# Loading the second batch's q and k ahead of a quarter of w_out, and transposing them in earlier slots

## The chip, the cores and the metric

The kernel runs on one core of a Trainium2 chip. The metric is the time of the whole kernel on the device in microseconds (us), as the median of several runs. The engines are named as the profile names them: PE is the TensorE matmul and PEld its weight load, DVE is VectorE, ACT is ScalarE, POOL is GpSimd and SP is SyncE. The last two mostly issue DMAs here.

## What is computed

Attention with a sliding window over 8 batches, 8 heads, 576 positions and a head size of 64, followed by a two-layer network with a piecewise activation on the 8 x 576 = 4608 tokens:

```python
scores = np.matmul(q, k.transpose(0, 1, 3, 2)) / np.sqrt(D)
mask = np.abs(pos[:, None] - pos[None, :]) <= 32
attn = softmax(np.where(mask, scores, -1e9))
x = np.matmul(attn, v).transpose(0, 2, 1, 3).reshape(B * S, H * D)   # 4608 x 512
h = x @ w_in                                                         # 512 x 2048
g = np.where(h >= 1, h, np.where(h <= -1, 0.0, (h + 1) ** 2 / 4))
out = g @ w_out                                                      # 2048 x 512
```

Inputs and output are float32; the matmuls take bfloat16, into which the loads cast.

## The kernel before, in words

All instructions are emitted by one Python program in a fixed order (`tc.manual_schedule()`), and each engine works through its own in that order. The order of the work is written by hand in the loop at L495, whose steps are called slots here. In slot `a` below 72, PE projects one tile of 256 tokens onto 256 of the 2048 columns of w_in (`project`, L486: 8 matmuls into a PSUM tile `hp`), ACT and DVE apply the activation and leave the result in `gT` (L532 to L540), and then PE does what else is planned for this slot: attention steps (`run(a)`), parts of the output product, and `run(a + 0.5)`. There are 8 slots to a token tile: slots 0 to 7 are tile 0, slots 8 to 15 tile 1, and slot 16 begins tile 2, the first whose `xT` holds tokens of the second batch.

Attention steps are put into slots by `at(a, ...)`. For one batch they are: `tposes` transposes q and k on PE, from the tiles `qn` and `kn` as loaded into PSUM tiles `tp`, which are then copied into `qT` and `kT`; `scores` (L213) adds the mask's bias by matmuls with `ident` (slots before 14), multiplies k and q and takes the exp on ACT into `pt`; `sums` (L267) multiplies the weights with v and with ones, takes the reciprocal by ln and exp on ACT, and leaves a multiply on DVE to be done at the next `flush`, which writes `xT`. PSUM tiles for these steps come from two pools, `ps_s` and `ps_n`, of one two-bank buffer each; `hp` has two buffers, so slot a needs the buffer of slot a-2. From the third batch on, q and k are transposed by DMAs on SP's queue (`xpose`), and only batches 0 and 1 use PE for it.

The activation has two forms. As a rule ACT does a relu into `rr`, DVE a maximum of `hp` and `rr`, and DVE a last operation; `hp` is free after the maximum. In slots of `two_on_act` (L382) ACT does relu and square, and DVE's single last operation (L537) reads `hp`, which is free only after that.

The first two token tiles use w_out in two halves of 256 columns, since w_out arrives late. The list `pairs` (L381) names the slot and the piece: piece x is half x//8 of the columns, tile x%8//4, and quarter x%4 of the 2048 rows (`pair`, L456: 8 matmuls). Pieces 0 to 3 are the left half of tile 0, piece 3 the last that needs w_out's rows k = 12 to 15 in blocks of 128. When four pieces are done ACT copies the sum to `osb` (L469) and SP stores it.

All loads but the first q are issued by POOL in the order of the `put` lists (L150 to L159). They use 8 semaphores in turn, so that a load waits at its issue until the load eight places earlier has landed.

`tposes(b, (t, half), (t, half))` (L325) makes four groups of transposes in two PSUM tiles. Each tile has two parts, of 5 and of 4 transposes per head pair (copies of 640 and of 512 columns). Before, ACT copies the first part of each tile and DVE the second.

Of the kernel before, what the change touches and what calls it, by code (L numbers as in the profile page):

```python
# [14 lines left out]
def kernel(  # L15
# [40 lines left out]
    ps_s = ctx.enter_context(tc.tile_pool(name="ps_s", bufs=1, space=bass.MemoryType.PSUM))  # L56
    ps_n = ctx.enter_context(tc.tile_pool(name="ps_n", bufs=1, space=bass.MemoryType.PSUM))
# [17 lines left out]
    V, P, A = nc.vector, nc.gpsimd, nc.scalar  # L75
# [68 lines left out]
    def put(todo):  # L144
        for fn, *x in todo:
            fn(*x)
# [2 lines left out]
    w = [(load_w_in, c0, c1, h) for c0, c1 in zip(cuts, cuts[1:]) for h in range(2)]  # L149
    put(w[:4] + [(load_half, 1, t, h) for t in range(2) for h in range(2)] + w[4:12])  # L150
    put([(load_w_out, 0, 0, 4)] + w[12:])
    put([(load_w_out, 0, k, k + 4) for k in range(4, 16, 4)] + [(load_rows, 1, t) for t in range(2)])
    put([(load_v, 1, n) for n in range(4)])
    P.tensor_copy(band[HD[1], 0:128], band[HD[1], 64:192])
    for m, n, x in ((mask4, 8, 128), (mask8, 4, TAIL)):
# [8 lines left out]
    def qkT(b, t):  # L164
        if t == 0:
            return qTs[b % 3][:, PAD:]
        if b not in kT:
            kT[b] = ktp.tile([128, NY * S], BF, name="kT")
        return kT[b]

    def tpose(b, n, t, copy, ps):


        half, part = divmod(n, 2)
        j0, j1 = ((0, 5), (5, 9))[part]
        if b:
            src = qn[b] if t == 0 else kn[b]
            src = [src[:, half + 2 * h] for h in range(2)]
            dst = qkT(b, t).rearrange("d (y e p j) -> d y e p j", y=2, e=2, j=9)[:, half, :, :, j0:j1]
            like = "d j (e p) -> d e p j"  # L180
        else:
            src = (qn, kn)[t][b, half]
            src = src if src.shape[1] == 9 else [src[:, h] for h in range(2)]
            dst = qkT(b, t).rearrange("d (y l p j) -> d l y p j", l=2, p=32, j=9)[:, half, :, :, j0:j1]
            like = "d j (p y) -> d y p j"
        for j in range(j0, j1):
            if isinstance(src, list):
                for h in range(2):
                    nc.tensor.transpose(ps[HD[h], j - j0], src[h][:, D * j:D * j + D], ident)  # L189
            else:  # L190
                nc.tensor.transpose(ps[:, j - j0], src[:, j], ident)
        return lambda: copy(dst, ps[:, :j1 - j0].rearrange(like, p=64 if b else 32))
# [132 lines left out]
    def tposes(b, *sets):  # L325

        todo = []
        for (t, half), pool in zip(sets, (ps_s, ps_n)):
            tp = pool.tile([128, 2, 8, 128], BF, name="tp", tag="bb")
            todo += [tpose(b, 2 * half + part, t, (A.copy, V.tensor_copy)[part], tp[:, part]) for part in range(2)]  # L330
        for copy in todo:
            copy()

# [44 lines left out]

    NB = NT // TB
    NF = DFF // 256  # L380
    pairs = [(6, 0), (7, 1), (8, 2), (9, 3), (11, 4), (12, 5), (15, 6), (15, 8), (16, 7), (17, 9)]  # L381
    two_on_act = (1, 7, 8, 9, 10, 11, 12)  # L382
    ev = {}

    def at(a, *todo):


        ev.setdefault(a, []).extend(x for x in todo if x)

    def steps(b, cut):  # L390

        for k, (lo, hi) in enumerate(((0, cut), (cut, MAIN))):
            for y1 in range(2):
                yield (sums, b, y1, lo, hi), (scores, b, (y1, y1 + 1), (0, 2), (2 * k, 2 * k + 2))
        yield (sums, b, 0, MAIN, S), (scores8, b)

    at(1, (tposes, 0, (0, 1), (1, 1)))
    at(2, (scores, 0, (0, 1), (0, 2), (2, 4)), (scores8, 0, ps_o))
    at(3, (scores, 0, (1, 2), (0, 2), (2, 4), ps_n), (sums, 0, 0, TB, MAIN, ps_s))
    at(4, (sums, 0, 1, TB, MAIN))  # L400
    at(5, (sums, 0, 0, MAIN, S, ps_s))
    seq = [x for b in range(1, B) for x in steps(b, 224)]
    at(13, seq[0][1])
    at(13.5, (*seq[1][1], ps_n))
    at(14, (*seq[0][0], ps_s), seq[1][0])
    at(16, seq[2][1])
    for n, a in enumerate((18, 20, 26.5, 28)):
# [5 lines left out]
    for n, a in enumerate(sl):  # L413
        at(a, seq[6 + n][0], seq[7 + n][1] if n < len(sl) - 1 else None)
    for t in range(2):
        at(11 + t, (tposes, 1, (t, 0), (t, 1)))
    loads, xps = {}, {16: [(2, 0)], 18: [(2, 1)]}
    for b in range(LONG + 1, B):
        a = sl[5 * (b - 1) - 7] - 17
# [53 lines left out]
    def run(pos):  # L473
        todo = []
        for fn, *x in ev.get(pos, []):
            if fn is sums:
                todo.append(sums(*x))
            elif fn is tposes:
                tposes(*x)
            else:  # L480
                pool = (x.pop(),) if x[-1] in (ps_s, ps_n, ps_o) else ()
                fn(*x, eng, *pool)
        for end in todo:
            end()
# [10 lines left out]
    for a in range(NF * NB + 2 * NF):  # L495
# [11 lines left out]
        if a < NF * NB:  # L507
            if wide:
                n, f = divmod(a - WIDE[0], 2 * NF)
                t = WIDE[0] // NF + 2 * n  # L510
# [6 lines left out]
            else:  # L517
                t, f = divmod(a, NF)
# [6 lines left out]
                elif not hps:  # L525
                    pool, tag = (ps_o, "op") if a == 6 else (ps_h, "hp")
# [60 lines left out]
```

The softmax here doesn't subtract the row's maximum and nothing guards it: scores larger than these inputs give would overflow.

## Time and profile before

| | us |
|---|---|
| median of 6 runs | 308.28 (307.87 to 308.71) |
| the profiled execution, its own time | 308.26 |
| its span, first to last instruction | 306.5 |
| PE busy | 298.1 (97%) |
| DVE busy | 240.4 (78%) |
| ACT busy | 191.5 (62%) |
| POOL busy | 77.0 (25%) |

The granted clock of TensorE is 0.999 of full speed over the span. The stretch of the change lies between 20 us (where POOL issues the loads concerned) and 47 us (slot 16). DMA queues are at 9 tenths or more in nearly every slice up to about 180 us and idle for most of the rest.

A timeline row gives start, length, engine, line, operation, output<-inputs, shape, the number of instructions merged into the row, and in brackets how long the engine stood idle before it and what released it. Lengths of neighbouring matmul rows overlap, since matmuls are pipelined; the distance from start to start is what a block costs. A row of the chain of waits gives start, length, and the instruction or wait on the path that set the end.

### The profile page before, as it was taken

How to read it: one execution, taken by the hardware profiler on the slowest of the kernel's cores; microseconds unless marked ns; L12 is line 12 of the kernel's file. 1: busy time of each engine (PE TensorE's matmuls, PEld its weight loads, DVE VectorE, ACT ScalarE, POOL GpSimd, SP SyncE). 2: the span in 40 equal slices, each digit the busy share in tenths (PEclk: the TensorE clock that was granted, in tenths of full speed). 3: DMA queues.
4: the chain of work that ended last, by engine and by line, in shares of the span. 5: the costliest groups of instructions: out<-in, count | busy, mean ns of one | idle time of the engine just before them, and what ended most of it. 6: DMA issues, size and time to landing. Idle time of an engine off the chain costs nothing.

```text
span 306.5 us, 7974 instructions
## 1 busy us (share of the span) xinstructions
PE 298.1 (97%) x3388; PEld 181.0 (59%) x3388; DVE 240.4 (78%) x376; ACT 191.5 (62%) x320; POOL 77.0 (25%) x92
## 2 busy tenths in 40 slices
PE   8889999999999999999999999999999999999995
PEld 3467778877666676666654544444445444446644
DVE  4278568888888989998999998888888888788700
ACT  3687886738856756776766766665667654444311
POOL 8797651037009009004600900000000000000000
PEclk9999999999999999999999999999999999999999
DMA  9999999999999999998999992550101000000121
GB/s 152 184 197 199 182 200 151 174 157 159 142 186 105 183 171 121 164 148 109 154 119 174 135 159 45 111 114 34 36 34 37 36 34 35 36 34 34 59 80 68
DMA packets 137171, 35.67 MB, mean 116 GB/s; under 512 B 122160, under 2 KB 132912, under 8 KB 137136
## 3 DMA queue, kind: packets, MB, share of 16 engines
q0 software_dynamic: 102976, 18.06, 83.5%
q1 hardware_dynamic: 34016, 16.81, 26.0%
q8 instruction: 26, 0.43, 0.6%
q10 hardware_dynamic: 144, 0.29, 0.4%
q14 instruction: 9, 0.07, 0.1%
HBM read 36.70 MB, written 9.44 MB: 151 GB/s over the span
## 4 chain that ended last, share of the span: by engine, by line
PE 90%; DMA 4%; POOL 3%; ACT 1%; issue 1%; DVE 0%; POOLq 0%; ACTq 0%
PE op L449 36%; PE hp L489 21%; PE hp L514 18%; PE bb L295 6%; PE op L464 4%; DMA w_in<-in_moe_w_in_dram 4%; PE bb L229 2%; POOL w_in L111 1%; PE op L440 1%; POOL vn L107 1%; PE tp L189 1%; ACT pt L237 1%; POOL kh L86 0%; DVE gT L537 0%; ACT mx L536 0%
## 5 line engine op out<-in xcount | busy, mean ns | idle before, releaser
L533 ACT ACTIVATE rr<-hp 128x512 f32<-128x512 f32 x144 | 85.6, 595 | 86.2 <-PE hp L489 41.8
L449 PE MATMUL op<-w_out,gT 128*128 128x512 bf16 x496 | 126.9, 380 | 0.0
L539 DVE TENSOR_TENSOR mx<-hp,rr 128x512 f32<-128x512 f32 x137 | 94.4, 689 | 25.7 <-ACT rr L533 23.9
L540 DVE SCALAR_TENSOR_TENSOR gT<-rr,mx 128x512 bf16<-128x512 f32 x137 | 94.8, 692 | 4.7
L489 PE MATMUL hp<-xT,w_in 128*128 128x256 bf16 x640 | 83.1, 273 | 2.6 <-DMA w_in<-in_moe_w_in_dram 1.2
L489 PEld LDWEIGHTS <-w_in 128*128 128x128 bf16 x640 | 61.9, 98 | 23.0 <-issue 3.3
L449 PEld LDWEIGHTS <-gT 128*128 128x128 bf16 x496 | 46.1, 98 | 45.2
L514 PE MATMUL hp<-xT,w_in 128*128 128x512 bf16 x256 | 65.7, 379 | 0.0
L514 PEld LDWEIGHTS <-w_in 128*128 128x128 bf16 x256 | 25.1, 98 | 30.2
L99 POOL DMA_DIRECT2D qn<-in_q_dram x12 | 14.6, 1221 | 89.9 <-DMA kT<-kn 87.9
L237 ACT ACTIVATE pt<-bb 128x1024 bf16<-128x1024 f32 (+1 forms) x33 | 32.7, 1002 | 4.5 <-PE bb L229 3.1
L107 POOL DMA_DIRECT2D vn<-in_v_dram x32 | 27.5, 888 | 4.6 <-DMA w_out<-in_moe_w_out_dram 3.6
L307 DVE TENSOR_TENSOR xT<-bb,rc 128x512 bf16<-128x512 f32 (+1 forms) x32 | 21.0, 657 | 9.7 <-ACT rc L302 8.8
L453 ACT COPY osb<-op 128x512 f32<-128x512 f32 x31 | 18.0, 581 | 11.4 <-PE op L449 11.1
L302 ACT ACTIVATE rc<-lr 128x512 f32<-128x512 f32 (+2 forms) x40 | 23.5, 587 | 1.3
L301 ACT ACTIVATE lr<-bb 128x512 f32<-128x512 f32 (+2 forms) x40 | 22.0, 551 | 0.4 <-PE bb L295 0.4
L203 DVE TENSOR_TENSOR pt<-pt,mask 128x1024 bf16<-128x1024 bf16 (+1 forms) x33 | 20.3, 614 | 0.5 <-ACT pt L237 0.5
L295 PE MATMUL bb<-pt,ones 64*64 64x256 bf16 (+3 forms) x352 | 19.5, 255 | 0.1
L295 PE MATMUL bb<-pt,vn 64*64 64x128 bf16 (+3 forms) x712 | 18.4, 204 | 0.2 <-DMA vn<-in_v_dram 0.2
L295 PEld LDWEIGHTS <-ones 64*64 64x64 bf16 x352 | 10.3, 105 | 11.6 <-issue 11.6
L295 PEld LDWEIGHTS <-vn 64*64 64x64 bf16 x712 | 16.7, 107 | 0.4 <-DMA vn<-in_v_dram 0.4
L464 PE MATMUL op<-w_out,gT 128*128 128x256 bf16 x128 | 16.5, 273 | 0.0
(61 smaller groups left out, 140.2 us busy)
## 6 DMA issues: line engine op xcount, KB each, us to landing
out_dram<-osb SPq DMA_DIRECT2D x35, 256.0 KB, 2.3
vn<-in_v_dram POOLq DMA_DIRECT2D x32, 144.0 KB, 10.0
qn<-in_q_dram POOLq DMA_DIRECT2D x12, 288.0 KB, 6.3
kn<-in_k_dram POOLq DMA_DIRECT2D x12, 288.0 KB, 9.0
w_in<-in_moe_w_in_dram POOLq DMA_DIRECT2D x12, 128.0 KB, 5.5
w_out<-in_moe_w_out_dram POOLq DMA_DIRECT2D x4, 256.0 KB, 8.1
w_out<-in_moe_w_out_dram POOLq DMA_DIRECT2D x2, 512.0 KB, 13.2
kh<-in_k_dram POOLq DMA_DIRECT2D x4, 144.0 KB, 5.2
```

The source lines that it names most:

```text
L107: nc.gpsimd.dma_start(out=vn[b][64 * a:64 * a + 64, :, h], in_=v[b, y:y + 2].rearrange("y s d -> (y s) d") .rearrange("(c r) d -> r c d", ...
L237: A.activation(p, ps[:, :, :w * n].rearrange(like, y=m), AF.Exp, scale=D ** -0.5)
L295: nc.tensor.matmul(bb[HD[h], a, o + c0:o + c1], ones[HD[a]] if c is None else vn[b][HD[a], c, h], p(a, h), start=n == 0, stop=True, skip_g ...
L301: A.activation(lr[:, :, :D0], bb[:, :, D0:2 * D0], AF.Ln)
L302: A.activation(rc[:, :, :D0], lr[:, :, :D0], AF.Exp, scale=-1.0)
L449: nc.tensor.matmul(op[tt], gT[:, j, home(tt // 2), 128 * (tt % 2):128 * (tt % 2) + 128], w_out[:, j], start=j == 0, stop=j == 15)
L464: nc.tensor.matmul(o[:, tt], gT[:, j, p, 128 * tt:128 * tt + 128], w_out[:, j, 256 * half:256 * half + 256], start=not done, stop=len(done ...
L489: nc.tensor.matmul(hp[:, j], w_in[:, kk, 256 * f + 128 * j:256 * f + 128 * j + 128], xT[:, kk, r0:r0 + TB], start=first and n == 0, stop=l ...
L514: nc.tensor.matmul(hp.rearrange("p n t -> p (n t)"), w_in[:, kk, 128 * f:128 * f + 128], xT[:, kk, r0:r0 + 2 * TB], start=n == 0, stop=n == 3)
L533: A.activation(rr, hp, AF.Relu, scale=0.5, bias=0.5)
L539: V.tensor_max(mx, hp, rr)
L540: V.scalar_tensor_tensor(g, rr, 1.0, mx, op0=ALU.min, op1=ALU.mult)
```

## The change

It does five things:

1. POOL issues the second batch's q and k (`load_rows`) ahead of w_out's last quarter of the left half (k = 12 to 15) instead of behind it. v stays where it was.
2. The second batch's transposes move from slots 11 and 12 to slot 10 (q) and 11.5 (k), that is, ahead of piece 4's matmuls by a slot, and behind them.
3. Piece 3 moves from slot 9 to slot 13, and slot 8 leaves `two_on_act`.
4. The first two scores of the second batch move from 13 and 13.5 to 12.5 and 13, so that slot 13's projection stands between them.
5. In `tposes`, ACT copies both parts of the first PSUM tile and DVE both parts of the second. This holds for the first batch's call in slot 1 too.

```diff
-    put([(load_w_out, 0, k, k + 4) for k in range(4, 16, 4)] + [(load_rows, 1, t) for t in range(2)])
+    put([(load_w_out, 0, k, k + 4) for k in (4, 8)] + [(load_rows, 1, t) for t in range(2)] + [(load_w_out, 0, 12, 16)])
...
-        for (t, half), pool in zip(sets, (ps_s, ps_n)):
+        for (t, half), pool, copy in zip(sets, (ps_s, ps_n), (A.copy, V.tensor_copy)):
             tp = pool.tile([128, 2, 8, 128], BF, name="tp", tag="bb")
-            todo += [tpose(b, 2 * half + part, t, (A.copy, V.tensor_copy)[part], tp[:, part]) for part in range(2)]
+            todo += [tpose(b, 2 * half + part, t, copy, tp[:, part]) for part in range(2)]
...
-    pairs = [(6, 0), (7, 1), (8, 2), (9, 3), (11, 4), (12, 5), (15, 6), (15, 8), (16, 7), (17, 9)]
-    two_on_act = (1, 7, 8, 9, 10, 11, 12)
+    pairs = [(6, 0), (7, 1), (8, 2), (11, 4), (12, 5), (13, 3), (15, 6), (15, 8), (16, 7), (17, 9)]
+    two_on_act = (1, 7, 9, 10, 11, 12)
...
-    at(13, seq[0][1])
-    at(13.5, (*seq[1][1], ps_n))
+    at(12.5, seq[0][1])
+    at(13, (*seq[1][1], ps_n))
...
-        at(11 + t, (tposes, 1, (t, 0), (t, 1)))
+        at(10 + 1.5 * t, (tposes, 1, (t, 0), (t, 1)))
```

On PE, block by block from slot 9's projection on (P is a slot's projection, `tq` and `tk` the transposes of q and k, sA and sB the two scores, uA and uB the two sums):

```
before  P9 pair3 P10 P11 tq pair4 P12 tk pair5 P13 sA sB P14 uA uB P15
after   P9 P10 tq P11 pair4 tk P12 pair5 sA P13 sB pair3 P14 uA uB P15
```

## The prediction

> **What bounds the kernel now.** I read the page first, then the chain of waits for 23 to 64 us, then the timelines of PE, ACT and DVE there.
>
> ```profile
> PE 298.1 (97%) x3388; PEld 181.0 (59%) x3388; DVE 240.4 (78%) x376; ACT 191.5 (62%) x320; POOL 77.0 (25%) x92
> ...
> PE 90%; DMA 4%; POOL 3%; ACT 1%; issue 1%; DVE 0%; POOLq 0%; ACTq 0%
> ```
>
> PE is the bound, so only idle time of PE can be won. Next, the chain (start, length, what):
>
> ```profile
> 17.10 6.95 DMA w_in<-in_moe_w_in_dram
> ...
> 24.18 1.03 PE hp L489 x8
> ...
> 31.89 0.61 ACT rr L533
> ...
> 32.52 0.64 ACT mx L536
> ...
> 33.19 0.70 DVE gT L537
> ...
> 33.93 1.03 PE hp L489 x8
> ...
> 41.78 1.95 ACT pt L237 x2
> ...
> 43.77 0.56 PE bb L295 x21
> ```
>
> Slot 5 (24.18) starts when its part of w_in lands, with 0.73 us of idle ahead of it on PE; whatever the change does before that has 0.73 us of cover. After it the chain leaves PE twice, both in the stretch that is changed, and after 48 us it is PE alone to the end. So PE's gain or loss at about 47 us is the gain or loss of the kernel. The PE timeline gives the distances (start, length):
>
> ```profile
> 31.69 1.04 PE L464 MATMUL op<-w_out,gT 128*128 128x256 bf16 x8
> 32.56 1.04 PE L489 MATMUL hp<-xT,w_in 128*128 128x256 bf16 x8
> 33.93 1.03 PE L489 MATMUL hp<-xT,w_in 128*128 128x256 bf16 x8 [0.33 <-DVE gT L537]
> 34.89 1.20 PE L189 MATMUL tp<-ident,qn 128*64 128x128 bf16 x36
> 36.02 1.05 PE L464 MATMUL op<-w_out,gT 128*128 128x256 bf16 x8
> ```
>
> Lengths overlap, so I count from start to start. A block of 8 takes 0.87 (31.69 to 32.56), or 0.96 where 64-wide work follows (33.93 to 34.89); 36 transposes take 1.13. By the same reading of the rows up to 44.26 (slot 15), three stalls stand there:
> - slot 11's projection comes 1.37 after slot 10's instead of 0.87: 0.50. It needs the PSUM buffer of slot 9, which in two_on_act slots is freed only by the DVE operation at the end (33.19+0.70).
> - the first scores take 0.68 (40.85 to 41.53), where slot 2's took 0.47: 0.21, for DVE's copies of kT.
> - the second sums start 0.68 after the first (43.09, 43.77), where the same 224-wide ones at 71.71 took 0.37: 0.31, for the second exp.
>
> Together 1.02 us, 0.33% of the span: nothing in this change can win more.
>
> **The loads.** No byte is added. By the landing times of the single issues, w_out's k=8..12 lands at 28.9 (20.5+8.4), its last quarter at 30.3, q at 33.1 (22.4+10.7), k at 36.0 (24.3+11.7): one after the other, 1.3, 2.9 and 2.9 apart. In the new order q lands at 31.8, k at 34.7, the quarter at 36.0, v as before. POOL's issues keep their places behind the waits for earlier w_in landings (q about 21.3, k 22.4, quarter 24.3); each move is past one or two issues of 0.75 us, and v's stay at 25.2.
>
> [...] By the row, q and k come 1.3 earlier; [...]
>
> **PE block by block, after.** Up to slot 9's projection (30.82) PE is as before. Slot 1's copies of batch 0 change too: DVE then copies 640+512 columns of k instead of 512+512, about 0.15 later, hidden by the 0.73.
> - Slot 10's projection moves up to 31.69, since pair 3 is gone. It needs slot 8's buffer; slot 8, off the two_on_act list, frees it at 30.14+0.60+0.69, about 31.5. No wait. That costs ACT 0.63 less and DVE 0.68 more, at a DVE that idles 1.05 in each of these slots: nothing.
> - q's transposes at 32.65: q has landed (31.8, margin 0.8).
> - Slot 11's projection could start at 33.78, and slot 9's DVE operation ends at 33.88 as before: 33.93, a stall of 0.15 left of the 0.50.
> - Pair 4 at 34.80, k's transposes at 35.77: k has landed (34.7, margin 1.0). But their tiles are q's: one buffer in each pool. ACT: slot 10's relu 33.06, square 33.69, then the two copies from 34.22, the second done about 35.5: the first tile is free. DVE: slot 10's operation 34.35 to 35.04, then both copies of the other tile.
>
> ```profile
> 36.17 1.39 ACT L192 COPY qT<-tp 128x640 bf16<-128x640 bf16 x2
> ...
> 36.94 1.38 DVE L192 COPY qT<-tp 128x512 bf16<-128x512 bf16 x2
> ```
>
> (ACT's and DVE's timelines, before.) DVE's 512-column copy takes 0.73, and the next follows after 0.65. A 640-column copy on DVE is in no row; with DVE's slope (448 to 512 columns of xT: 0.62 to 0.69, 1.04 ns each) I take 0.86, next after 0.78. [...] By the row the second copy ends at 36.51, [...] The second 18 transposes could start at 36.33 and wait to 36.56: a new stall of 0.23. Queued behind it on PE is everything after it.
> - Slot 12's projection at 37.13, pair 5 at 38.00 (its gT from slot 11 is done about 37.35), first scores at 38.97, their kT part at 39.21; DVE's two kT copies end about 38.8. The old stall of 0.21 is gone with 0.3 to spare.
> - Scores are now parted by slot 13's projection, which adds two switches between 64-wide and 128-wide work: 0.35 instead of 0.23 behind the first, 0.97 instead of 0.87 ahead of the second: 0.2 us of new cost.
> - Slot 13 at 39.56, second scores 40.52, pair 3 at 41.11 (w_out landed at 36.0; even behind v, at 41.0, it would not wait), slot 14 at 41.99, sums 42.96 and 43.33. The exps run 39.65 and 41.2 to 42.2: the stall of 0.31 is gone. The output copy of tile 0 moves from 33.1 to 42.2 on ACT, ahead of slot 14's relu (43.06), in idle time; its buffer is needed by pair 8 at 45.6. Its store passes nothing on SP's queue.
> - Slot 15 at 43.82, against 44.26.
> - Slot 16 needs xT from ACT's ln and exp chain: from the first ln to the end of the last multiply 3.0 us (44.09 to 47.10). From 43.6 it ends at 46.6, where slot 16's third matmul would be at 46.67. It just fits.
>
> Sum: -1.02 of stalls, +0.15 +0.23 left or new, +0.20 of switches: -0.44 us. The profiled execution took 308.26 (span 306.5 and 1.76 around it), the median is 308.28: **307.8**. About 0.2% (0.62 us) is what a measurement of this kernel tells from no change, so this counts as within: below 307.66 is faster, above 308.90 slower.
>
> **Rivals.**
> - Full gain: the tiles are free in time (DVE's copies 0.12 shorter each), so 0.23 less: -0.67, 307.6. For it: ACT's half is free in time. Against: every 512 copy on DVE took 0.71 to 0.73. Chance 0.25, with what else could be better than my sum.
> - The loads do not do what they say: with transfers sharing, q stays at 33.1 and k at 36.0. Then the q transposes start at 33.2, slot 11 at 34.36 (0.43 late), k's second half no longer waits (0.23 back): -0.24, 308.0. Likewise a gain half lost on ACT. Against: landings in order. Chance 0.12, between 308.0 and 308.4.
> - Slower: one engine now copies a tile's two halves in a row. If DVE's copies are longer by d than I take, k's second half waits 2d longer, and the kT copies come 4d later, against a kT read that itself slipped by 2d and has 0.3 to spare: loss 4d-0.3. The gain is gone at d = 0.2, and it is slower by over 0.62 from d = 0.35, a 640 copy of 1.2. At d = 0.4 it is +0.86, 309.1. For it: the page shows DVE the busiest after PE (78%). Against: in this stretch it idles 1 us in each slot, and the four copies there kept 0.72 to 0.73 beside POOL's issues. Chance 0.13.
> - My sum, 307.7 to 308.05, has 0.50.
>
> Faster 0.25, within 0.62, slower 0.13. For 8 in 10 I take 307.4 to 308.7: it reaches past the full gain (0.67, and 0.2 for unknown costs) and over the lost one, and leaves out the slower case.
>
> **What would show it.** In the new profile: PE's idle at slot 11 about 0.15 with the same releaser; a wait of k's transposes for DVE's copy of qT, near 36.5; none for a DMA; no wait of scores or sums for ACT or DVE; slot 15's projection near 43.8; the same tail after it. I am wrong if transposes wait for q or k, if slot 16 waits for xT, or if PE after 48 us has idle time that it had not.

## The result, and the profile after

The changed kernel takes 307.72 us (median of 17 runs, 307.41 to 308.19) against 308.39 us (37 runs, 307.78 to 309.15) for the kernel before, measured beside it: a ratio of 0.998 (95% interval 0.9974 to 0.9987), that is 0.4 to 0.8 us less. Forecast were 307.8 and a gain of 0.44, about two thirds of the 0.67 between the medians. That 307.72 comes so near 307.8 is in part luck: the forecast counted from 308.28, the median of the first six runs, and over 37 runs the kernel before has 0.11 more. The gain, not the time, is what the forecast has to be held against. By its own bounds the forecast called 307.66 to 308.90 "within", and 307.72 lies there, close to the edge.

The page of the changed kernel, the lines that answer to those of before. The engines' shares hardly move:

```profile
PE 298.6 (98%) x3388; PEld 181.3 (59%) x3388; DVE 241.0 (79%) x377; ACT 190.8 (62%) x319; POOL 77.2 (25%) x92
...
PE 90%; DMA 4%; POOL 3%; issue 1%; ACT 1%; DVE 0%; POOLq 0%; ACTq 0%
```

The chain of waits of the changed kernel from 23 to 64 us (start, length, what):

```profile
17.56 6.84 DMA w_in<-in_moe_w_in_dram
...
24.53 1.03 PE hp L489 x8
...
33.53 0.70 DVE gT L537
...
34.28 1.03 PE hp L489 x8
35.31 0.87 PE op L464 x8
36.18 1.30 PE tp L189 x36
37.49 0.98 PE hp L489 x8
...
43.30 0.85 PE bb L295 x48
44.15 0.98 PE hp L489 x8
```

In this execution w_in landed 0.35 later than in the profiled one before (slot 5 starts at 24.53, not 24.18), ahead of all that the change moves in the loads; so the two are compared from slot 5's projection (the 8 matmuls with which slot 5 begins) on. The chain now leaves PE once instead of twice: slot 11 still waits for DVE, and the exps (41.78 before) are off it, the sums standing in one piece of 0.85. PE's timeline after:

```profile
31.17 1.91 PE L489 MATMUL hp<-xT,w_in 128*128 128x256 bf16 x16
33.01 1.20 PE L189 MATMUL tp<-ident,qn 128*64 128x128 bf16 x36
34.28 1.03 PE L489 MATMUL hp<-xT,w_in 128*128 128x256 bf16 x8
35.15 1.04 PE L464 MATMUL op<-w_out,gT 128*128 128x256 bf16 x8
36.11 1.38 PE L189 MATMUL tp<-ident,kn 128*64 128x128 bf16 x36
37.42 1.05 PE L489 MATMUL hp<-xT,w_in 128*128 128x256 bf16 x8
...
44.08 1.05 PE L489 MATMUL hp<-xT,w_in 128*128 128x256 bf16 x8
...
46.71 1.04 PE L489 MATMUL hp<-xT,w_in 128*128 128x256 bf16 x8
47.68 0.42 PE L229 MATMUL bb<-qT,kT 64*64 64x128 bf16 x16
```

The rows of before that the last ones answer to, slot 15's projection, slot 16's, and slot 16's scores:

```profile
44.26 1.05 PE L489 MATMUL hp<-xT,w_in 128*128 128x256 bf16 x8
...
46.89 1.08 PE L489 MATMUL hp<-xT,w_in 128*128 128x256 bf16 x8
47.90 0.42 PE L229 MATMUL bb<-qT,kT 64*64 64x128 bf16 x16
```

In the timeline after, the first row is slots 9 and 10, now without a piece between them. From q's transposes to slot 11 it takes 1.27, where 36 transposes take 1.13: 0.14 is left of the 0.50. k's transposes take 1.31: 0.18 of new wait. Slot 15 starts 19.55 behind slot 5; before it was 20.08 (24.18 to 44.26). Slot 16's scores start 23.15 behind slot 5, before 23.72 (24.18 to 47.90): 0.57 us won. From there to the start of the last matmul both take the same, 254.89 us before and 254.87 after. **In this pair of profiles all of the gain lies between slot 5 and slot 16**, and this distance, D, is what the experiments are read by: in all of them the rest is 254.87 to 254.89.

One part of the change acts ahead of slot 5, where D doesn't see it: the copies of slot 1. In slot 2 of the changed kernel the first scores' matmuls wait for DVE's copy of kT:

```profile
19.58 0.41 PE L208 MATMUL bb<-bias,ident 64*64 64x512 bf16 x4
20.07 0.42 PE L229 MATMUL bb<-qT,kT 64*64 64x128 bf16 x16
```

They start 0.49 behind the bias matmuls, and 0.24 in the kernel before. The 0.25 is more than the 0.15 that was forecast, but PE still idles 0.41 for w_in ahead of slot 5, so it is covered here as forecast. The wait is not there in every execution: e3, e4, e6 and e8, which have the new copies too, are without it, and e2, with the old ones, has 0.14.

### The profile page after: what moved, and what is told of

Read it like the earlier page. It is cut to its first block, busy times and chain, and to the rows that moved or that the text cites. A ratio compares the mean times of both kernels' runs of the same rounds, so it can differ in the third digit from the quotient of the medians.

```text
span 306.2 us, 7973 instructions
## 1 busy us (share of the span) xinstructions
PE 298.6 (98%) x3388; PEld 181.3 (59%) x3388; DVE 241.0 (79%) x377; ACT 190.8 (62%) x319; POOL 77.2 (25%) x92
## 4 chain that ended last, share of the span: by engine, by line
PE 90%; DMA 4%; POOL 3%; issue 1%; ACT 1%; DVE 0%; POOLq 0%; ACTq 0%
PE op L449 36%; PE hp L489 21%; PE hp L514 18%; PE bb L295 6%; PE op L464 5%; DMA w_in<-in_moe_w_in_dram 4%; PE bb L229 2%; POOL w_in L111 1%; PE op L440 1%; POOL vn L107 1%; PE tp L189 0%; POOL kh L86 0%; DVE gT L537 0%; PE bb L208 0%; ACT mx L536 0%
## 5 line engine op out<-in xcount | busy, mean ns | idle before, releaser
L302 ACT ACTIVATE rc<-lr 128x512 f32<-128x512 f32 (+2 forms) x40 | 23.5, 587 | 1.3
```

Of the source, the lines that this page charges most:

```text
L302: A.activation(rc[:, :, :D0], lr[:, :, :D0], AF.Exp, scale=-1.0)
```

## The experiments

D has a resolution of some hundredths (from slot 5's projection to slot 9's it is 6.63 to 6.64 in the eight profiles in which no load of w_out holds PE up), where the times of a kernel's runs spread by 0.3 to 1.8 us. But each D is one execution. It is taken from times before rounding, so the last digit can differ by one from the rows.

| kernel | D, us | median, us | ratio to before (95%) |
|---|---|---|---|
| before | 23.72 | 308.39 | |
| changed | 23.15 | 307.72 | 0.998 (0.9974 to 0.9987) |
| e1, loads back | 23.83 | 308.33 | 1.0004 (0.9992 to 1.0015) |
| e2, copies by part | 23.40 | 307.58 | 0.9977 (0.9969 to 0.9985) |
| e3, slot 8 back on the list | 23.36 | 308.04 | 0.9987 (0.998 to 0.9993) |
| e4, slot 9 off the list | 22.93 | 307.66 | 0.9974 (0.9964 to 0.9985) |
| e5, before with slot 9 off | 23.24 | 307.94 | 0.9989 (0.9979 to 0.9999) |
| e6, e4 and scores together | 23.06 | 307.31 | 0.9964 (0.9951 to 0.9976) |
| e7, e6 and copies by part | 22.66 | 307.24 | 0.9965 (0.9953 to 0.9978) |
| e8, e1 and e4 | 23.51 | 308.08 | 0.9993 (0.9982 to 1.0004) |

The kernel before ran again beside e1 to e4 (308.40) and beside e5 to e8 (308.42). Each kernel's gain in the median agrees with its gain in D to about 0.2 us, when the delays that are named below for e2 and e6 are taken out of D.

**e1: are the earlier loads needed?** The changed kernel with the loads in the old order:

```diff
-    put([(load_w_out, 0, k, k + 4) for k in (4, 8)] + [(load_rows, 1, t) for t in range(2)] + [(load_w_out, 0, 12, 16)])
+    put([(load_w_out, 0, k, k + 4) for k in range(4, 16, 4)] + [(load_rows, 1, t) for t in range(2)])
```

> The changed kernel with the loads alone in the old order (w_out's last quarter of the left half ahead of q and k); slots, pieces and copies stay as changed. Distance from slot 5's projection to slot 16's scores on PE: 23.72 us before, 23.15 us after. My theory (landing order is issue order, and the stalls are PE's): q lands about 9.0 us behind slot 5's start instead of 7.4, so q's transposes wait for the DMA by about 0.55 us, slot 11 loses its 0.14 of waiting for DVE, the second half of k's transposes its 0.18: distance 23.4, time about +0.25 us against the changed kernel, -0.3 against before, still a gain. Rival (the earlier loads are the whole of it): 23.7 or more, time as before or slower.

The whole gain is gone: D 23.83, the time that of before. Both are the rival's figures, and not my 23.4; only the trace separates the two. The wait that I had named is there, but it is longer. PE's timeline, its list of waits, and the load of q (issued at 23.5) in this run:

```profile
34.14 1.20 PE L189 MATMUL tp<-ident,qn 128*64 128x128 bf16 x36 [0.93 <-ACT rr L533]
```

```profile
PEld L189 <- DMA qn<-in_q_dram: 1.2, 1, 1.2
```

```profile
L93 POOL DMA_DIRECT2D qn<-in_q_dram x1: 747/747/747, 23.5 to 23.5; - x1
...
DMA to landing us min/median/max: 10.6/10.6/10.6
```

The first row names ACT, whose tile had long been free; the weight load in the second shows the true releaser, q's DMA. q landed at 34.1, 9.4 us behind slot 5 (24.67), not 9.0 as in the profile before: in this execution w_out's first quarter landed 1.5 us behind the w_in load ahead of it, against 0.8 to 0.9 in both profiles of the result, and everything queued behind was later. That is not the loads' order, for the quarter is ahead of all that was reordered. The wait for q was 1.0 instead of the 0.55 that I had set. That the earlier loads are the whole of the gain does not follow: e5 gains 0.48 of D without them. e8 shows the case with the loads in time.

**e2: does it matter which engine copies what?** The changed kernel with the copies as before:

```diff
-        for (t, half), pool, copy in zip(sets, (ps_s, ps_n), (A.copy, V.tensor_copy)):
+        for (t, half), pool in zip(sets, (ps_s, ps_n)):
...
-            todo += [tpose(b, 2 * half + part, t, copy, tp[:, part]) for part in range(2)]
+            todo += [tpose(b, 2 * half + part, t, (A.copy, V.tensor_copy)[part], tp[:, part]) for part in range(2)]
```

> The changed kernel with the copies alone as before (ACT the first part of each PSUM tile, DVE the second). My theory (what counts is when DVE, which starts last, is done): DVE then copies 512 and 512 columns instead of 640 and 512 and is done about 0.1 us earlier, so the second half of k's transposes waits about 0.1 us instead of 0.18, but the first tile is now free only after DVE's first copy, about when k's transposes begin: distance from slot 5 to slot 16's scores 23.05 to 23.15, time -0.1 to 0 us against the changed kernel. Rival (a tile that one engine copies is what makes room for k's transposes): the first half waits for DVE too, both stalls together 0.4 us or more, time +0.2 us or more.

D is 23.40, but 0.30 of it stands elsewhere. Here too w_out's first quarter was late (1.6 us behind w_in), and the second quarter behind it, which slot 7's piece needs, held PE up. The chain of this run begins there:

```profile
20.21 8.73 DMA w_out<-in_moe_w_out_dram
28.94 0.04 issue
...
30.02 0.87 PE hp L489 x8
```

In PE's timeline the piece of slot 7 starts 1.17 behind its projection (28.99, 27.82) instead of 0.87. Without that, D is 23.10, as reckoned, not measured. k's transposes, by PE's timeline of the same run:

```profile
36.55 1.33 PE L189 MATMUL tp<-ident,kn 128*64 128x128 bf16 x36
37.82 1.05 PE L489 MATMUL hp<-xT,w_in 128*128 128x256 bf16 x8
```

1.27 instead of 1.31: the wait is 0.14 and not 0.18, as DVE's two copies are shorter (1.38 together by its timeline, against 1.45 in the changed kernel). The time can't be told from the changed kernel's (307.58 and 307.72, overlapping intervals). So one engine to a tile is not what brings the gain; by these rows it costs 0.04 in this stretch.

**e3: why did slot 8 leave the list?**

```diff
-    two_on_act = (1, 7, 9, 10, 11, 12)
+    two_on_act = (1, 7, 8, 9, 10, 11, 12)
```

> The changed kernel with slot 8 alone back in the list of slots with two operations on ACT. My theory (a buffer of hp is held until the last read of it): slot 10's projection waits for slot 8's last DVE operation, a stall of 0.45 to 0.5 us with DVE as releaser, of which slot 11's 0.14 and about 0.15 of the wait of k's transposes are given back: distance 23.35, +0.2 us against the changed kernel. Rival (the list only balances ACT and DVE, which idle here anyway): no new wait, distance 23.15.

As expected, D 23.36. PE's timeline shows the old wait one slot earlier, at slot 10 for slot 8's buffer:

```profile
31.03 1.04 PE L489 MATMUL hp<-xT,w_in 128*128 128x256 bf16 x8
32.39 1.03 PE L489 MATMUL hp<-xT,w_in 128*128 128x256 bf16 x8 [0.33 <-DVE gT L537]
33.35 1.20 PE L189 MATMUL tp<-ident,qn 128*64 128x128 bf16 x36
34.48 1.05 PE L489 MATMUL hp<-xT,w_in 128*128 128x256 bf16 x8
```

Slots 9 and 10 stand 1.36 apart, 0.49 too much, and slot 11 (1.13 behind q's transposes) waits no more. Balancing ACT and DVE is not what the list does here: it sets how long a PSUM buffer is held.

**e4: can slot 11's rest go the same way?**

```diff
-    two_on_act = (1, 7, 9, 10, 11, 12)
+    two_on_act = (1, 7, 10, 11, 12)
```

> The changed kernel with slot 9 alone taken off the list of slots with two operations on ACT. My theory: slot 9's buffer is free 0.6 us earlier, so slot 11's wait of 0.14 goes; ACT does slot 10's square 0.3 us earlier, so DVE's copies of q end 0.3 us earlier and the wait of k's transposes (0.18) goes or nearly goes: distance 22.8 to 22.9, time -0.3 us against the changed kernel, -0.85 against before. Rival (DVE, with one operation more in slot 9, becomes late for q's copies and the wait of k's transposes grows by 0.3): distance 23.3, +0.15 us.

D is 22.93. PE's timeline:

```profile
32.88 1.20 PE L189 MATMUL tp<-ident,qn 128*64 128x128 bf16 x36
34.00 1.05 PE L489 MATMUL hp<-xT,w_in 128*128 128x256 bf16 x8
...
35.85 1.29 PE L189 MATMUL tp<-ident,kn 128*64 128x128 bf16 x36
37.08 1.05 PE L489 MATMUL hp<-xT,w_in 128*128 128x256 bf16 x8
```

Slot 11's 0.14 is gone, and k's transposes take 1.23, 0.10 of wait for 0.18. DVE's copies of q began 0.2 earlier, counted from slot 5 (34.94 behind 24.40, against 35.29 behind 24.53), not 0.3, and k's transposes themselves came 0.14 earlier. The time, 307.66, can't be told from the changed kernel's, and its median is 0.06 below, where I had forecast 0.3; the gain of 0.22 is read from D alone.

**e5: is that one number enough without the rest?** The kernel before, with slot 9 off its list:

```diff
-    two_on_act = (1, 7, 8, 9, 10, 11, 12)
+    two_on_act = (1, 7, 8, 10, 11, 12)
```

> The kernel before with slot 9 alone taken off the list of slots with two operations on ACT, nothing else. My theory: slot 11's wait of 0.50 us goes and nothing takes its place (q and k land 1 us or more ahead of their transposes in the old slots), so the distance from slot 5's projection to slot 16's scores falls from 23.72 to 23.2 and the time by 0.5 us, nearly what the whole change gave. Rival (the later stalls at the scores and sums grow by what slot 11 wins, since DVE has one operation more): 23.5 to 23.7, time within 0.2 us of before.

D 23.24 as expected, though I had the inside wrong. Its chain:

```profile
36.26 0.69 DVE gT L537
36.95 0.69 DVE qT L192
37.64 0.04 issue
37.69 1.34 PE tp L189 x36
...
41.51 1.93 ACT pt L237 x2
```

Slot 11's 0.50 and the 0.21 at the first scores are gone, but k's transposes, now earlier, wait for DVE's copies of q: 1.09 behind slot 12 instead of 0.96, and 0.14 more in their middle. The second sums still wait for the second exp. Something did take its place, 0.27 us of it. Even so, this single number is worth 0.48 of D, where the whole change is worth 0.57. Its medians differ by 0.48 too, but the times alone are barely clear of no change (0.9979 to 0.9999).

**e6: what does the projection between the scores cost?** e4 with

```diff
-    at(13, (*seq[1][1], ps_n))
+    at(12.5, (*seq[1][1], ps_n))
```

> The changed kernel with slot 9 off the list and both first scores in 12.5, so that no projection parts them. My theory: the two switches between 64-wide and 128-wide work go (0.2 us), kT and both exps are in time all the same: distance 22.73, -0.2 us against the run with slot 9 off alone (22.93). Rival (the parting is what gives ACT time for the second exp): the second sums wait for it as before the change, 0.2 to 0.3 us, distance 22.9 to 23.0.

D reads 23.06, since w_out's second quarter held PE up here too, behind a first quarter that landed 1.9 us behind w_in. It shows in slot 7 (PE's timeline):

```profile
27.39 1.04 PE L489 MATMUL hp<-xT,w_in 128*128 128x256 bf16 x8
28.63 1.03 PE L464 MATMUL op<-w_out,gT 128*128 128x256 bf16 x8 [0.20 <-DMA w_out<-in_moe_w_out_dram]
```

The distance is 1.24 instead of 0.87, so the load accounts for 0.37; D reckoned without that is 22.69, about the expected 0.2 below e4. The second sums follow the first after 0.38 (42.86, 43.24): the exp was in time, and the parting (slot 13's projection between the two scores) wasn't needed for it.

**e7: the copies by part on top.** The edit of e2 on e6.

> The run before this one (slot 9 off, both scores in 12.5) with the copies by part as before the change. My theory: the wait of k's transposes, 0.09 us with slot 9 off, falls to about 0.05 or nothing, since DVE copies 512 and 512 columns: distance 22.65 to 22.73. Rival (the tile's one engine makes room): 0.2 us more, 22.9.

D 22.66, with no late DMA: 1.06 below before and the lowest of all. k's transposes take 1.17 (35.61 to 36.78), 0.04 of wait. Its median, 307.24, is the lowest here, 0.9965 of before (0.9953 to 0.9978), but can't be told from e6's 307.31.

**e8: the old loads with slot 9 off.** The edits of e1 and e4 together.

> The changed kernel with slot 9 off the list and the loads in the old order. My theory: q's landing decides when q's transposes begin, so slot 9's edit, worth 0.2 us with the new loads, is worth nothing here: distance 23.4 if q lands 9.0 us behind slot 5's start (as in the kernel before), 23.8 if at 9.4 (as in the run with the loads back); time as that run, 308.3. Rival (the loss with the loads back was something else than the wait for q): 0.2 us faster than it.

```profile
33.69 1.20 PE L189 MATMUL tp<-ident,qn 128*64 128x128 bf16 x36 [0.59 <-DMA qn<-in_q_dram]
34.82 1.05 PE L489 MATMUL hp<-xT,w_in 128*128 128x256 bf16 x8
```

In PE's timeline the wait for q stands by name. q landed 9.1 behind slot 5 (at 33.6, issue 22.7 and 10.9), and D is 23.51, 0.36 above the changed kernel. It is also what e1 comes to when the 0.32 by which its q was later is taken out (9.42 and 9.10 behind slot 5). Slot 11 follows q's transposes without a wait, so slot 9's edit wins nothing here. The medians, 308.33 and 308.08, differ by about what the rival had forecast, but their intervals overlap, so they don't decide between the theories; the wait for q in the traces does.

## Why the prediction held, step by step

- **PE sets the end, and only the stretch up to slot 16 counts.** Shown: the rest is 254.87 to 254.89 in all ten profiles.
- **Loads.** By its landing times the changed kernel has q at 32.0 (7.4 behind slot 5; forecast 31.8 minus 24.18 is 7.6), k at 34.9, w_out's quarter at 36.2, one after the other as taken. In none of the ten profiles did a later one of these loads land first. The rival's supposition, that transfers share and q lands no earlier, was not shown: q came 1.6 nearer to slot 5 (7.4 behind it, 9.0 before). The wait for q that the rival priced at about 0.55 (32.65 to 33.2) is real once the order is undone (1.0 in e1, 0.66 in e8); the rival's gain was 0.24, and e8, where slot 9's edit wins nothing, gives 0.21. So the new order is needed for the new slots.
- **Slot 10** had no wait; the removal of slot 8 from the list carries it (e3).
- **Slot 11**: 0.15 forecast, 0.14 measured. **k's transposes**: 0.23 forecast, 0.18 measured. The term that was off is the 640-column copy on DVE, which the trace of before did not hold. The changed kernel's copies of q, by DVE's timeline and by the source line:

```profile
35.29 1.45 DVE L192 COPY qT<-tp 128x640 bf16<-128x640 bf16 x2
```

```profile
L192 DVE COPY qT<-tp x2: 722/768/815, 35.3 to 36.0; 128x640 bf16<-128x640 bf16 x1, 128x512 bf16<-128x512 bf16 x1
```

It took 0.815 us; I had 0.86. The forecast took its slope, 1.04 ns a column, from another operation (xT's multiply of float32; the means over the whole trace of before, 623 ns for 448 columns and 691 for 512, give 1.06); between these two copies it is 0.73 ns a column. Both copies together took 1.45, forecast 1.51. They end at 36.74, and the second half of k's transposes starts at 36.79, so the releaser that was forecast is the right one.
- **Scores, sums**: no wait was left, and the switches cost what was said (e6: about 0.2, by D without its late load).
- **The sum** was 0.44, the trace says 0.57. Of the 0.13, 0.05 is k's transposes, 0.04 the other blocks from slot 11 to slot 15 (9.80 for the 9.89 of my list, with those 0.05), and 0.04 a short wait of slot 16 for xT in the kernel before (1.01 from slot 16's projection to its scores, after it 0.97), which I did not count as a stall. The runs' interval, 0.4 to 0.8, holds both numbers.
- **The rival of the full gain** had 0.67, which is just the difference of the medians, so the times do not rule it out. Its mechanism is out: it had the tiles free in time, and k's transposes still wait 0.18.
- **The rival of slow copies on DVE** is out: they were shorter than taken (0.815 for 640 columns, taken as 0.86).

What stays open: why w_out's first quarter lands late in some executions (1.5 to 1.9 us behind w_in in e1, e2 and e6, 0.8 to 1.1 us in the other seven profiles). It is upstream of the change and costs 0.3 to 0.4 us when it strikes. The traces show where it arises: between 18 and 24 us the DMAs moved less in just these three. The kernel before, then e1, by the DMA view of this stretch:

```profile
DMA packets 1884, 1.19 MB, mean 199 GB/s; under 512 B 97, under 2 KB 1883, under 8 KB 1883
```

```profile
DMA packets 1510, 1.01 MB, mean 168 GB/s; under 512 B 80, under 2 KB 1509, under 8 KB 1509
```

e2 has 177 and e6 175 GB/s, the other seven profiles 198 to 200; from 12 to 18 us all ten have 196 to 199. What slowed the DMAs no run here tells. It may be part of why runs of one kernel spread: these three profiled executions took 0.3 to 0.9 us more than the medians of their kernels, the other seven from 0.1 less to 0.3 more.

Open too is what the moves of the transposes and of piece 3 are worth each by itself: no run takes back one of them alone.

## What to carry to other kernels

Where one engine is busy to 97%, list the places where it starts later than the block ahead takes, and change only those; here they summed to 1.02 us. The kernel with the shortest D (e7) still has 0.04 of wait and is 1.06 of D below the one before, slightly more than the list held, since slot 16's 0.04 was not on it and other blocks are some hundredths shorter. A PSUM buffer was free here only after its last read: a form of the operation that reads it late stalled the producer two steps on (0.50 at slot 11 in the kernel before, 0.49 at slot 10 in e3) though both consumers idled (ahead of slot 9's operations in the kernel before, ACT 0.48 and DVE 1.05), and one number in a list (e5) gave most of what moving loads, transposes, scores and copies gave together (0.48 of 0.57, by D). When something is moved to an earlier slot, read from the landing times whether its load has room: in the old order the transposes were safe in slot 11 and would not have been in slot 10.

## What the runs showed that was not expected

The same load, in the same place of the order, lands up to 1 us later in some executions (w_out's first quarter 0.8 behind w_in in the changed kernel, 1.9 in e6), so a margin in one trace is not the same in every run. For q it was forecast as 0.8, and was 1.0 in the profile of the changed kernel; in e2, with the late quarter, q landed at 33.1 and its transposes began at 33.4, and in e6 the margin was 0.4 too.
